# Two spectral-mixing and two GEGLU layers on one core: every pair of f tiles of w_down as seven block products

## The chip, the cores and the metric

The kernel is one program on one core of a Trainium2 chip. The metric is device time in microseconds (us) of one execution, as the median of several runs. Besides these runs one execution was recorded by the hardware profiler; all durations below that are not medians come from that execution.

The engines are named as in the profile: PE (TensorE's matrix multiplications), PEld (its weight loads), DVE (VectorE), ACT (ScalarE), POOL (GpSimd, which also issues DMAs) and SP (SyncE, which issues most DMAs).

## The reference

The input x has 2048 rows (S) and 512 columns (D), all in fp32. Four layers follow, each added to x after a layer norm without weights:

```python
def _A_ref(x, ...):              # Real(DFT_seq(DFT_hidden(x)))
    a = einsum("bsd,ed->bse", x, dft_hid_re)
    b = einsum("bsd,ed->bse", x, dft_hid_im)
    return einsum("ts,bse->bte", dft_seq_re, a) - einsum("ts,bse->bte", dft_seq_im, b)

def _B_ref(x, w_gate, w_up, w_down):          # F = 1792
    return (_gelu(x @ w_gate) * (x @ w_up)) @ w_down

x = x + _A_ref(_layernorm(x), ...)
x = x + _B_ref(_layernorm(x), ...)
x = x + _A_ref(_layernorm(x), ...)
x = x + _B_ref(_layernorm(x), ...)
```

## The kernel before

**Arithmetic.** An fp32 tile is split into a high and a low part (`split`: ACT copies to fp32r, DVE subtracts), and one product of two tiles is three matmuls: high times high, high times low, low times high (`mm3`, lines 175 to 177 of the profile). Each streams 512 columns through a 128x128 weight tile. Where a product can be cut in 2x2 blocks, the kernel takes seven block products and some sums in place of eight. The block products have names of their own: A11, A12, A22 of the weights themselves and S1 to S4 of sums of them.

**Layers.** `mix(layer)` for layers 0 and 2 goes over four column blocks b of the sequence transform, each in stages: A11 and A12 (for all four b first), then for each b S2 (which also makes S1 and S3), EARLY_HID, S4, MID_HID and LATE_HID. `six` is one block product of these stages: six matmuls, then one `step()`. `geglu(w, layer)` for layers 1 and 3 does half w of the rows (1024 rows, as two parts of 512). For each f tile n of 14, `up(n)` computes gate and up by block products, and GELU times up gives the hidden tile `h`. The product with w_down is either

* plain: for each f tile, part and 128 rows three matmuls (`down_steps`, `plain_rows`), that is 48 matmuls for a pair of f tiles, or
* by pairs: two neighbouring f tiles are one 2x2 block matrix with the two parts, and `down_product` does seven block products of six matmuls, that is 42 matmuls for a pair. A11 and A12 run beside `up` (`beside`), the others after it, in the order of `down_order`.

`SEVEN` says how many of the seven pairs of a layer and half are done by pairs. Before it is

```python
SEVEN = {(1, 1): 5, (3, 0): 7, (3, 1): 5}
```

so the half (layer 1, w 0) is plain altogether, (1, 1) and (3, 1) have five pairs and four plain f tiles, and (3, 0) has seven pairs.

**Rows.** A product by pairs yields transposed column blocks. `ended` closes an accumulation; `turned_rows` transposes on DVE and adds to the rows, which `load_turned` had loaded as `xwide` (part 0) and `wide` (part 1), and `rows_done` stores them with four DMAs a part. Where plain f tiles follow, the rows are stored to a buffer `begun` instead, loaded again in plain layout, and `plain_rows` adds the rest with `x_add`. After (1, 1) `plain_rows` keeps these tiles for the next layer norm (`keep`), so layer 2 does not load its second half of rows.

**Weights of the pairs.** `weight_steps(k, wdc, wdd)` loads pair k of w_down, makes four sums of 128x256 on DVE, splits four pieces and stores seven tiles to `wc`. Each product later loads its own tile from there (`s<-wc`). Before, pairs 0 and 1 are queued at the end of (1, 0), pairs 2 to 6 are made during `up` of (1, 1). The plain f tiles have split copies of their own (`wd`), made in (1, 0).

**What sets the order.** The kernel traces its work in one order: `queue` holds small steps of which each product runs one (`step`), `chores` are spread over the eight groups of a HID stage (`hid_groups`, `chores_at`), `slow` runs one step in nine. A stream of weight tiles (`items`, `take`) loads and splits a few items ahead. Tiles come from 94 slots of 128x512 (`s`), and the two wide tiles are lent to the same pool. The scheduler of the compiler then orders each engine's instructions. Within an engine the order is fixed: an instruction that waits holds up everything behind it on its engine.

Of the kernel before, what the change touches and what calls it, by code (L numbers as in the profile page):

```python
# [9 lines left out]
F32 = mybir.dt.float32  # L10
# [24 lines left out]
NSLOT = 94  # L35
SEVEN = {(1, 1): 5, (3, 0): 7, (3, 1): 5}
FORE = {0: 4, 2: 4}
MADE = 5
LEAD = 3
NK = NS // 2  # L40
# [6 lines left out]
def fnet_geglu(ctx: ExitStack, tc: tile.TileContext, x_in, ws, wh, wgu, wdn, wdc, out):  # L47
# [211 lines left out]

    items = []  # L260
    stream = {"loaded": 0, "split": 0, "used": 0, "more": 0}
    raws, parts = {}, {}

    def load_next():
        n = stream["loaded"]
        dtype, addresses, _, _ = items[n]
        raws[n] = []
        for a in addresses:
# [173 lines left out]
    for layer in range(0, 4, 2):  # L442
        mix_items(layer)
        for w in range(NB // 2):
            if (layer + 1, w) not in SEVEN:
                for part in range(2):
                    for f in range(NF):
                        if layer == w == part == 0:
                            items.append((F32, (wdn[f],), make_down_first(f), None))
                        else:  # L450
                            items.append((F32R, halves(wds[f]), whole, NEAR[0]))
            else:
                for near, products in zip(NEAR[1:], down_order(layer + 1, w)):
                    items.extend((F32R, (down_piece(k, name),), whole, near) for name, k in products)
                items.extend((F32R, halves(wds[f]), whole, NEAR[2]) for f in range(2 * SEVEN[layer + 1, w], NF))

# [207 lines left out]
    def mix(layer):  # L664
        hid, sums, chores, hid_left = {}, {}, [], [0]

        def chores_at(b):
            if b == NB - 3:
# [169 lines left out]
    def weight_steps(n, raw=wgu, place=wblocks):  # L838
# [19 lines left out]
        def divide(i):  # L858
            def run():
# [7 lines left out]
                if place is wblocks:  # L867
                    piece_here(n, i, t)
                else:
                    sb.put(*t)  # L870
                sb.put(src[i])
# [4 lines left out]
    def down_weight_steps(k):  # L876
        return weight_steps(k, wdc, wdd)

    down_making = {}
# [27 lines left out]
    def geglu(w, layer):  # L907
# [147 lines left out]
        def prepared(name, k):  # L1055

            if (name, k) in bs:
                return
            if k >= MADE:
                if name == "S1":  # L1060
                    second_made(k)
                elif name == "S2":
                    fourth_made(k)
            t = h4[k][PLACE[name]]
# [80 lines left out]

        def turned_rows(part, c, src):

            t = sb.get()
            blocks_of = "p (j e) -> p j e"
            nc.vector.transpose(t.rearrange(blocks_of, e=32), src.rearrange(blocks_of, e=32))  # L1150
            to = xturned[part].rearrange("p (j c e) -> p j c e", c=NT, e=32)[:, :, c]
            plus(to, to, t.rearrange(blocks_of, e=32))
            sb.put(t)

        def rows_done(part):
            rows_moved(layer + 1, part, lambda v, outside: nc.gpsimd.dma_start(outside, v))

        xrows = []
# [14 lines left out]
        def plain_rows():  # L1173
# [6 lines left out]
            for i in range(2 * NT):  # L1180
                part, n = divmod(i, NT)
                if part == 0:
                    ready(fs[n], 1)
# [44 lines left out]
        if w == 0:  # L1228
            queue.extend(others)
            if layer == 1:  # L1230
                down_making.update((k, down_weight_steps(k)) for k in range(2))
                queue.extend([down_making[0][0], down_making[1][0], *down_making.pop(0)[1]])
        elif before_mix:
# [19 lines left out]
        else:  # L1253
            if pairs == NP:
                pair_combined(NP - 1)
            late = down_order(layer, w)[1]
            for i, (name, k) in enumerate(late):
                for more in late[i:i + EARLY + 1]:
# [11 lines left out]
                while w == 0 and len(queue) > 2 * (len(late) - 1 - i):  # L1270
                    step()
            if pairs < NP:
                plain_rows()
# [4 lines left out]
        elif before_mix:  # L1278
            queue.extend([lambda k=k: combine_late(k) for k in range(NK)])

# [110 lines left out]
```

## Time and profile before

| | |
|---|---|
| median of 3 runs (lowest to highest) | 1619.23 us (1619.18 to 1620.68) |
| the profiled execution's own time | 1620.1 us |
| its span, first to last instruction | 1618.3 us |
| mean granted TensorE clock | 0.999 |
| busy share PE / DVE / ACT / POOL | 99% / 72% / 51% / 14% |
| DMA, read and written | 336.86 MB and 85.72 MB |

PE's busy time is a union of modelled, overlapping matmuls: it tells that PE rarely stands still, and the distance between the starts of two matmuls tells its pace. A row of the groups gives the source line, engine, operation, output<-input by the program's names, the shape, the count, then the busy time and the mean duration, then the engine's idle time ahead of these instructions and what ended it. A row of the windows has, for each engine, the busy time in this stretch and the instructions.

### The profile page before, as it was taken

To read this page: it belongs to the slowest core of one execution; us is meant where nothing else is said; L and a number is where in the kernel's file an instruction comes from. 1 tells how busy PE (TensorE), PEld (TensorE's weight loads), DVE (VectorE), ACT (ScalarE), POOL (GpSimd) and SP (SyncE) were. 2 spreads that over 40 slices of the span, in tenths; PEclk is the share of its full clock that TensorE was granted. 3 is DMA by queue.
4 is the path that set the end of the run, shared out by engine and by line. 5 is a ranking of instruction groups with operands and counts; after the bars stand their busy time and mean duration, and the time that the engine had idled before them with its cause. 6 is when DMAs were issued, how large, how long until landed. Compare 5 with 4: busy or idle time off the path is not lost.

```text
span 1618.3 us, 22864 instructions
## 1 busy us (share of the span) xinstructions
PE 1607.9 (99%) x7066; PEld 1325.5 (82%) x7066; DVE 1172.0 (72%) x2009; ACT 827.3 (51%) x1605; POOL 229.0 (14%) x421
## 2 busy tenths in 40 slices
PE   9999999999999999999999999999999999999998
PEld 6888888888888888888888888888888888888886
DVE  8999878888876655657877987887854547854573
ACT  7754454544775535557585434545445535433360
POOL 2101010203544022220131000100000000000002
PEclk9999999999999999999999999999999999999999
DMA  9858778799978799977858777777989676995455
GB/s 357 283 205 305 244 256 268 241 319 372 331 257 281 242 349 360 346 255 234 290 162 297 248 254 227 273 236 278 288 271 309 193 221 198 296 298 178 130 176 156
DMA packets 252106, 424.15 MB, mean 262 GB/s; under 512 B 28816, under 2 KB 91024, under 8 KB 250960
## 3 DMA queue, kind: packets, MB, share of 16 engines
q1 hardware_dynamic: 227232, 336.95, 65.1%
q0 software_dynamic: 24752, 85.74, 14.2%
q8 instruction: 56, 0.92, 0.3%
q14 instruction: 66, 0.54, 0.1%
HBM read 336.86 MB, written 85.72 MB: 261 GB/s over the span
## 4 chain that ended last, share of the span: by engine, by line
PE 95%; DMA 2%; DVE 1%; ACT 0%; issue 0%; POOL 0%; SPq 0%; POOLq 0%; DVEq 0%
PE p L177 32%; PE p L176 31%; PE p L175 31%; PE p L728 1%; DVE s L142 1%; DMA out<-s 1%; DMA s<-begun 0%; ACT s L141 0%; DMA begun<-xwide 0%; DMA s<-t 0%; DMA s<-x 0%; DVE s L166 0%; DVE s L1150 0%; DVE xwide L166 0%; DVE s L163 0%
## 5 line engine op out<-in xcount | busy, mean ns | idle before, releaser
L176 PE MATMUL p<-s,s 128*128 128x512 f32 x2334 | 907.5, 389 | 0.0
L177 PE MATMUL p<-s,s 128*128 128x512 f32 x2334 | 898.3, 389 | 0.4 <-DVE s L142 0.4
L175 PE MATMUL p<-s,s 128*128 128x512 f32 x2334 | 891.1, 389 | 0.1
L141 ACT ACTIVATE s<-s 128x512 fp32r<-128x512 f32 (+1 forms) x760 | 434.3, 606 | 387.1 <-DVE s L163 82.4
L142 DVE TENSOR_TENSOR s<-s,s 128x512 fp32r<-128x512 f32 (+1 forms) x760 | 481.0, 662 | 110.7 <-ACT s L141 82.2
L177 PEld LDWEIGHTS p<-s,s 128*128 128x128 f32 x2334 | 438.2, 188 | 92.7 <-DVE s L142 0.8
L175 PEld LDWEIGHTS p<-s,s 128*128 128x128 f32 x2334 | 438.2, 188 | 92.0 <-ACT s L141 1.0
L176 PEld LDWEIGHTS p<-s,s 128*128 128x128 f32 x2334 | 438.2, 188 | 92.0 <-issue 0.5
L166 DVE TENSOR_TENSOR s<-s,p 128x512 f32<-128x512 f32 x303 | 202.6, 682 | 176.4 <-PE p L177 94.1
L163 DVE TENSOR_TENSOR s<-s,s 128x512 f32<-128x512 f32 (+1 forms) x313 | 188.2, 614 | 16.3 <-DMA s<-ws 9.1
L170 ACT ACTIVATE s<-p 128x512 f32<-128x512 f32 x217 | 126.3, 591 | 120.1 <-PE p L177 117.9
L904 ACT ACTIVATE s<-s 128x512 f32<-128x512 f32 x104 | 65.4, 629 | 84.0 <-DVE s L166 82.5
L141 ACT ACTIVATE s<-xwide 128x512 fp32r<-128x512 f32 (+1 forms) x91 | 55.7, 618 | 54.2 <-PE p L176 22.3
L142 DVE TENSOR_TENSOR s<-xwide,s 128x512 fp32r<-128x512 f32 (+1 forms) x91 | 61.1, 676 | 21.8 <-ACT s L141 12.5
L498 POOL TENSOR_SCALAR rstd<-rstd 128x1 f32<-128x1 f32 x48 | 18.0, 376 | 388.7 <-ACT s L497 270.2
L166 DVE TENSOR_TENSOR s<-s,s 128x512 f32<-128x512 f32 (+1 forms) x61 | 37.4, 615 | 25.5 <-DMA s<-ws 14.3
L918 DVE TENSOR_TENSOR s<-s,s 128x512 f32<-128x512 f32 x77 | 53.1, 690 | 1.9
L257 POOL DMA_DIRECT2D wb<-s x84 | 45.7, 545 | 47.8 <-ACT s L141 28.7
L219 POOL DMA_DIRECT2D x<-s x43 | 23.5, 547 | 177.8 <-DVE s L166 176.3
L517 ACT ACTIVATE s<-s,shift,rstd 128x512 f32<-128x512 f32 x55 | 43.9, 808 | 7.2 <-DVE shift L490 6.2
L495 ACT ACTIVATE s<-s 128x512 f32<-128x512 f32 x39 | 24.3, 624 | 38.2 <-DMA s<-x 20.7
L599 DVE STREAM_TRANSPOSE wide<-s 128x512 f32<-128x512 f32 x29 | 20.3, 705 | 24.0 <-ACT s L517 24.0
(109 smaller groups left out, 524.8 us busy)
## 6 DMA issues: line engine op xcount, KB each, us to landing
s<-ws SPq DMA_DIRECT2D x375, 256.0 KB, 4.2
s<-wb SPq DMA_DIRECT2D x294, 256.0 KB, 4.6
s<-wc SPq DMA_DIRECT2D x119, 256.0 KB, 4.1
s<-wh SPq DMA_DIRECT2D x114, 256.0 KB, 4.9
wb<-s POOLq DMA_DIRECT2D x98, 256.0 KB, 4.5
s<-x SPq DMA_DIRECT2D x67, 256.0 KB, 4.9
xwide<-ws SPq DMA_DIRECT2D x56, 256.0 KB, 4.4
wc<-s POOLq DMA_DIRECT2D x49, 256.0 KB, 5.4
```

Of the source, the lines that this page charges most:

```text
L141: nc.scalar.activation(hi, src, AF.Copy)
L142: nc.vector.tensor_tensor(lo, src, f32(hi), op=ALU.subtract)
L163: nc.vector.tensor_tensor(out, a, b, op=ALU.subtract)
L166: nc.vector.tensor_tensor(out, a, b, op=ALU.add)
L170: nc.scalar.activation(v, src, AF.Copy)
L175: nc.tensor.matmul(ps, ah, bh, start=start, stop=False, skip_group_check=True)
L176: nc.tensor.matmul(ps, ah, bl, start=False, stop=False, skip_group_check=True)
L177: nc.tensor.matmul(ps, al, bh, start=False, stop=stop, skip_group_check=True)
L257: nc.gpsimd.dma_start(a, f32(t))
L517: nc.scalar.activation(z, x, AF.Identity, bias=shift, scale=rstd)
L904: nc.scalar.activation(t, g, AF.Gelu_apprx_tanh)
L918: nc.vector.tensor_tensor(t, t, v, op=ALU.mult)
```

## The change

All four entries of `SEVEN` become 7, so every pair of f tiles in both GEGLU layers and both halves is done by block products. With it:

* No plain f tile is left: `wd` is neither made nor loaded, and `plain_rows` and `begun` are not used any more.
* The weights of the pairs have to be ready for (1, 0). Pairs 0 and 1 are made among the chores of block b = 0 of layer 0 and pairs 2 and 3 among those of b = 1 (`BEFORE`, `down_chores`); pairs 4 to 6 during `up` of (1, 0).
* After (1, 1) the rows are stored by `rows_done` and loaded again for layer 2 from POOL's queue (`second_rows`). These steps and the sums that follow are spread over A11 and A12 of layer 2 (`GAPS`: empty steps between them).
* At the end of the program (`last_rows`) the product A22 runs one column block after the other: all seven pairs of block c = 0, then of c = 1, and each is transposed and added in two halves of 256; the rows leave in eight DMAs from SP as the halves are done.

```diff
-SEVEN = {(1, 1): 5, (3, 0): 7, (3, 1): 5}
+SEVEN = {(1, 0): 7, (1, 1): 7, (3, 0): 7, (3, 1): 7}
+BEFORE = {0: (0, 1), 1: (2, 3)}
+GAPS = 1, 2, 1
...
         def chores_at(b):
+            return (down_chores(*BEFORE.get(b, ())) if layer == 0 else []) + other_chores(b)
...
+    def down_chores(*ks):
+        steps = [down_weight_steps(k) for k in ks]
+        return [load for load, _ in steps] + [run for _, runs in steps for run in runs]
...
         def up(n):
-            if layer == 1 and w == 1:
+            if layer == 1 and w == 0:
                 k, odd = divmod(n + 3, 2)
-                if not odd and 2 <= k < NP:
+                if not odd and sum(map(len, BEFORE.values())) <= k < NP:
                     down_making[k] = down_weight_steps(k)
                     down_making[k][0]()
...
+        def last_rows():
+            ks, chain = range(pairs), banks["chain"]
+            ts = [take()[0] for _ in ks]
+            for k in ks:
+                prepared("A22", k)
+            for c in range(2):
+                for t, k in zip(ts, ks):
+                    weights = (t[:, h][:, c * P:(c + 1) * P] for h in half)
+                    mm3(chain[c], weights, bs["A22", k], False, k == pairs - 1)
+                for cut in half:
+                    turned_rows(0, 2 + c, chain[c], cut)
+                    if c:
+                        js = slice(cut.start // 32, cut.stop // 32)
+                        rows_moved(layer + 1, 0, lambda v, outside: nc.sync.dma_start(outside[:, js], v[:, js]))
...
-            queue.extend([lambda k=k: combine_late(k) for k in range(NK)])
+            if pairs == NP:
+                lend("x")
+                lend("z")
+                for k in (*range(NT, NK), *range(NT)):
+                    queue.extend([lambda k=k: second_rows(layer + 1, k), *[None] * GAPS[0]])
+                for k in range(NK):
+                    queue.extend([lambda k=k: combine(k), *[None] * GAPS[1]])
+            for k in range(NK):
+                queue.extend([lambda k=k: combine_late(k), *[None] * GAPS[2]])
```

PE's list gets shorter by 66 matmuls of 512 columns (7021 rows become 6955). Behind the added lines the line numbers are higher by 2 to 36: `mm3` is lines 177 to 179, the additions of line 166 are line 168, the transposes of line 1150 are line 1160. Three places show how the instructions move.

DVE in layer 0, block b = 0, between EARLY_HID and S4. Before, it holds splits (L142, L159) and the sums for the next S2 (L163, L166), all of 128x512:

```order
L159 SCALAR_TENSOR_TENSOR s_1902<-s_1691,s_1901 128x512
L166 TENSOR_TENSOR s_1869<-s_1867,s_1869 128x512
L142 TENSOR_TENSOR s_1928<-xwide,s_1927 128x512
L163 TENSOR_TENSOR s_1867<-s_1871,s_1867 128x512
L166 TENSOR_TENSOR s_1891<-s_1889,s_1891 128x512
```

In the changed kernel the same stretch has the four sums of one pair of w_down between them (128x256, on the tiles s_1747 to s_1750, which a DMA from `wdc` fills):

```order
L161 SCALAR_TENSOR_TENSOR s_1903<-s_1689,s_1902 128x512
L168 TENSOR_TENSOR s_1749<-s_1750,s_1749 128x256
L165 TENSOR_TENSOR s_1748<-s_1747,s_1750 128x256
L144 TENSOR_TENSOR s_1919<-xwide,s_1918 128x512
L168 TENSOR_TENSOR s_1892<-s_1890,s_1892 128x512
L161 SCALAR_TENSOR_TENSOR s_1925<-s_1691,s_1924 128x512
L165 TENSOR_TENSOR s_1748<-s_1749,s_1747 128x256
```

The sums of the weights now stand ahead of splits that PE needs for the next stages of layer 0.

POOL from the end of (1, 1) to the start of layer 2. Before, it stores `begun`, and then the tiles of `plain_rows` (x of layer 2), with no load:

```order
L1156 DMA begun_1_0_6741<-xwide 32x16x128 x4
L1156 DMA begun_1_1_6742<-wide 32x16x128 x4
L219 DMA x_2_94<-s_8757 128x512
L219 DMA x_2_94<-s_8759 128x512
L219 DMA x_2_94<-s_8761 128x512
```

In the changed kernel the rows themselves go out (x_3 is part 1, x_2 part 0) and come back on the same queue, with the terms of the norms (`rstd`) between them:

```order
L1166 DMA x_3_95<-wide 32x16x128 x4
L205 DMA s_8981<-x_3_95 128x512
L205 DMA s_9025<-x_3_95 128x512
L205 DMA s_9069<-x_3_95 128x512
L205 DMA s_9113<-x_3_95 128x512
L1166 DMA x_2_94<-xwide 32x16x128 x4
L499 TENSOR_SCALAR rstd<-rstd 128x1 x2
```

The eight loads of rows are new on this queue, and each group of four has to wait for the store ahead of it to land.

DVE at the end of the program. Before, the last instructions are additions of whole tiles from PSUM (p), each of which releases a store:

```order
L166 TENSOR_TENSOR wide<-wide,s_16542 128x16x32
L166 TENSOR_TENSOR s_16615<-s_16615,p_16657 128x512
L166 TENSOR_TENSOR s_16617<-s_16617,p_16672 128x512
L166 TENSOR_TENSOR s_16619<-s_16619,p_16687 128x512
L166 TENSOR_TENSOR s_16621<-s_16621,p_16702 128x512
```

In the changed kernel the last ones are transposes and additions of halves, first of one PSUM bank (p_15194, column block c = 0) and then of the other (p_15195, c = 1):

```order
L168 TENSOR_TENSOR wide<-wide,s_16705 128x16x32
L1160 STREAM_TRANSPOSE s_16763<-p_15194 128x256
L1160 STREAM_TRANSPOSE s_16766<-p_15194 128x256
L168 TENSOR_TENSOR xwide<-xwide,s_16763 128x8x32
L168 TENSOR_TENSOR xwide<-xwide,s_16766 128x8x32
L1160 STREAM_TRANSPOSE s_16790<-p_15195 128x256
L1160 STREAM_TRANSPOSE s_16797<-p_15195 128x256
L168 TENSOR_TENSOR xwide<-xwide,s_16790 128x8x32
L168 TENSOR_TENSOR xwide<-xwide,s_16797 128x8x32
```

The work behind the last matmul becomes four instructions on halves, and then the stores from `xwide`.

More of the change, by code (lines that the diff above doesn't have):

```diff
@@ L257, in kept @@
             nc.gpsimd.dma_start(a, f32(t))
-    items = []
+    items, needs, outside = [], {}, set()
     stream = {"loaded": 0, "split": 0, "used": 0, "more": 0}
@@ L267, in load_next @@
         raws[n] = []
+        assert n not in needs or needs[n] in outside
         for a in addresses:
@@ L444, in fnet_geglu @@
         for w in range(NB // 2):
[L445 to L455, printed above, removed]
+            for near, products in zip(NEAR[1:], down_order(layer + 1, w)):
+                for name, k in products:
+                    needs[len(items)] = k, next(i for i, names in enumerate(pieces) if name in names)
+                    items.append((F32R, (down_piece(k, name),), whole, near))
+            for f in range(2 * SEVEN[layer + 1, w], NF):
+                if layer == 0:
+                    items.append((F32, (wdn[f],), make_down_first(f), None))
+                else:
+                    items.append((F32R, halves(wds[f]), whole, NEAR[2]))
     queue, slow, steps_done = [], [], [0]
@@ L869, in run @@
                 else:
+                    outside.add((n, i))
                     sb.put(*t)
@@ L1058, in prepared @@
                 return
[L1059 to L1063, printed above, removed]
+            if name in ("S1", "S2") and len(h4[k]) == 4:
+                second_made(k)
+            if name == "S2" and k >= MADE:
+                fourth_made(k)
             t = h4[k][PLACE[name]]
@@ L1181, in plain_rows @@
                 part, n = divmod(i, NT)
-                if part == 0:
+                if part == 0 and n < len(fs):
                     ready(fs[n], 1)
@@ L1229, in geglu @@
             queue.extend(others)
-            if layer == 1:
-                down_making.update((k, down_weight_steps(k)) for k in range(2))
-                queue.extend([down_making[0][0], down_making[1][0], *down_making.pop(0)[1]])
         elif before_mix:
@@ L1256, in geglu @@
             late = down_order(layer, w)[1]
+            last = layer == 3 and w == 1
+            if last:
+                late = late[:-pairs]
             for i, (name, k) in enumerate(late):
@@ L1271, in geglu @@
                     step()
-            if pairs < NP:
+            if last:
+                last_rows()
+            elif pairs < NP:
                 plain_rows()
```

10 lines of the change are left out of this document (6 added, 4 removed).

## The prediction

> **What bounds the kernel now.** I read the page first, then PE's waits, then PE's timeline where its starts are not evenly spaced, then the groups and the windows of the stretches that the change touches, and last the chain at the end.
>
> The page: span, busy times, DVE in 40 slices, and the chain by engine:
>
> ```profile
> span 1618.3 us, 22864 instructions
> PE 1607.9 (99%) x7066; PEld 1325.5 (82%) x7066; DVE 1172.0 (72%) x2009; ACT 827.3 (51%) x1605; POOL 229.0 (14%) x421
> ...
> DVE  8999878888876655657877987887854547854573
> ...
> PE 95%; DMA 2%; DVE 1%; ACT 0%; issue 0%; POOL 0%; SPq 0%; POOLq 0%; DVEq 0%
> ```
>
> The chain that sets the end is PE from start to end. DVE comes next, and it is at 90% or more in the first mixing layer (slices 1 to 3) and around slice 19. The list of all that PE waited for is three rows long, which says that nearly every producer is early:
>
> ```profile
> PE p L1285 <- POOL ident masks.py:199: 1.4, 1, 1.4
> PE p L728 <- ACT s L517: 1.2, 1, 1.2
> PE p L177 <- DVE s L142: 0.4, 1, 0.4
> ```
>
> So a matmul that is not there any more is worth its distance to the next one. PE's timeline at the end, first and last of 13 matmuls in a row:
>
> ```profile
> 1607.85 0.39 PE L177 MATMUL p<-s,s 128*128 128x512 f32 x1
> ...
> 1610.57 0.39 PE L177 MATMUL p<-s,s 128*128 128x512 f32 x1
> ```
>
> Twelve distances in 2.72 us are 0.2267 us each. The 0.39 us is the latency of one matmul, and is not what is saved.
>
> **The change part by part.**
>
> *Fewer matmuls.* A pair costs 42 matmuls in place of 48, six less. New pairs are seven in (1, 0), two in (1, 1) and two in (3, 1): 11 x 6 = 66 matmuls, and PE's list shows just these 66 gone. 66 x 0.2267 = **-15.0 us**. The trace's 226.7 ns is used here. The Trainium skill's "TensorE: Matmul & The Clock Gate" (section "Wait — 56ns, not 53.3ns?") gives 215.7 ns between the starts of warm matmuls of 512 columns; by it, as an estimate, the term would be -14.2 us, and the trace is 5% slower than it.
>
> *plain_rows goes.* Two starts in it come late; and one at the hand-over from (3, 0), which already has seven pairs:
>
> ```profile
> 793.08 0.39 PE L177 MATMUL p<-s,s 128*128 128x512 f32 x1
> 793.52 0.50 PE L175 MATMUL p<-s,s 128*128 128x512 f32 x1
> ...
> 797.07 0.39 PE L176 MATMUL p<-s,s 128*128 128x512 f32 x1
> 797.88 0.50 PE L177 MATMUL p<-s,s 128*128 128x512 f32 x1 [0.42 <-DVE s L142]
> ...
> 1390.13 0.61 PE L175 MATMUL p<-s,s 128*128 128x512 f32 x2
> 1390.79 0.50 PE L176 MATMUL p<-s,s 128*128 128x512 f32 x1
> ```
>
> The first two gaps are 0.44 and 0.81 us, 0.8 us over the pace together, and go with `plain_rows`: **-0.8 us**. The third is 0.2 us over it (0.66 us for two matmuls less 0.45). (1, 0) gets the same hand-over: **+0.2 us**, and at most some 3 us, because DVE has more to do there (below).
>
> *The making of the weights moves.* Per pair it is three loads on SP, four half sums on DVE, three whole splits and a half one on ACT and DVE, and seven stores on POOL. The rows for the prices, then the windows of layer 0 from b = 0's S2 on, of (1, 0), of layer 2's A11 with A12, of its first S2, and of (3, 0):
>
> ```profile
> L142 DVE TENSOR_TENSOR s<-s,s 128x512 fp32r<-128x512 f32 x696 | 457.7, 684 | 104.7 <-ACT s L141 76.4 <-PE p L176 8.2 <-PE p L177 7.2
> L163 DVE TENSOR_TENSOR s<-s,s 128x256 f32<-128x256 f32 x83 | 33.2, 418 | 5.0 <-ACT s L517 4.6
> L166 DVE TENSOR_TENSOR s<-s,s 128x256 f32<-128x256 f32 x16 | 6.7, 420 | 11.0 <-DMA s<-wgu 7.9 <-DMA s<-wdc 3.2
> L141 ACT ACTIVATE s<-s 128x512 fp32r<-128x512 f32 x696 | 412.9, 625 | 380.3 <-DVE s L163 81.3 <-PE p L176 67.5 <-PE p L177 51.7
> ```
>
> ```profile
> 100.00:260.00 160.00, 160.00 (x708) 132.53 (x707) 141.75 (x233) 79.79 (x148) 18.20 (x35) 1.00 0.76 255
> 402.00:613.00 211.00, 211.00 (x933) 174.77 (x932) 144.22 (x258) 119.90 (x243) 72.57 (x138) 1.00 0.85 296
> 820.00:903.00 83.00, 83.00 (x367) 68.64 (x366) 66.72 (x123) 52.81 (x113) 16.91 (x22) 1.00 0.69 228
> 903.00:936.00 33.00, 33.00 (x147) 27.34 (x146) 30.80 (x52) 16.08 (x29) 1.08 (x2) 1.00 0.80 253
> 1208.00:1405.00 197.00, 196.95 (x870) 162.67 (x869) 120.82 (x190) 101.78 (x192) 7.42 (x17) 1.00 0.80 241
> ```
>
> Busy time by count gives what one costs in a dense queue: 457.7 / 696 = 0.66 us for a whole DVE operation, 0.40 for a half one, and 0.59 us for a whole one on ACT (a half one is taken at 0.40, too). A pair is 5 x 0.40 + 3 x 0.66 = 4.0 us of DVE, four pairs 16 us. The first sum also waits for the raw weights, and all of DVE's queue behind it with it: 11.0 us in 16 such rows, 0.7 us each, so 3 us for four. That makes 19 us. From 100 to 260 us DVE has 160 - 141.75 = 18.2 us free, and PE does not wait there. The work just fits, and what is late spills into the stretch after it, where the page's slices show 80%. POOL (18 of 160 us busy) takes 28 stores of 0.52 us (18.20 / 35), and the 9 MB of DMA are 57 GB/s on top of 255, below the peaks that the trace has elsewhere (296 as a mean over (1, 0)). I take **0**; the bounds are 0 and the second rival.
>
> *(1, 0) and (1, 1).* Seven pairs in (1, 0) need 11 whole DVE operations each (four sums, seven splits): 51 us; three pairs are made there: 12 us. The plain version's 28 splits of `h` and 14 of w_down (28 us) and the making of two pairs (8 us) go. DVE goes from 144 of 211 us to 171 of about 202. (3, 0) runs the same product code without a real gap, at 121 of 197. **0**, at most the 3 us named. (1, 1) loses the making of five pairs, and gains nothing but two pairs. SP's list has 77 loads from `wc` more, and 44 from `wd` and 14 of w_down less, of 256 KB each; (3, 0) shows the loads from `wc` hidden.
>
> *Rows come back from outside.* The same trip stands in the chain of the last stage:
>
> ```profile
> 1586.66 0.29 POOL begun L1156
> ...
> 1595.02 3.18 DMA s<-begun
> ...
> 1598.30 0.70 DVE s L166
> ```
>
> From the first store to the first use it takes 11.6 us. In the new order 175 matmuls, 39.7 us, lie between the last A22 product and the first A12 product of layer 2, which wants these rows; product k = 7 is 42 matmuls later, 49.2 us in all. ACT has 66 whole and 16 half operations in these 49.2 us: 66 x 0.59 + 16 x 0.40 = 45 us. DVE has 144 whole and 48 half ones up to the end of the first S2, 511 matmuls or 115.8 us: 144 x 0.66 + 48 x 0.40 = 114 us. Both fit, without room. Nothing in the trace shows this fit itself; the nearest row is the window 903 to 936, where DVE is busy for 30.8 of 33 us and PE does not wait. Between 0 and 7.6 us (first rival) I take **+1.0 us**.
>
> *The end.* The DMA issues' sizes and times to landing (stores of plain rows, loads of turned ones), the transpose out of PSUM among the groups, and two runs of four issues in SP's timeline:
>
> ```profile
> out<-s SPq DMA_DIRECT2D x8, 256.0 KB, 4.4
> xwide<-x SPq DMA_DIRECT2D x21, 256.0 KB, 8.0
> ```
>
> ```profile
> L1150 DVE STREAM_TRANSPOSE s<-p 128x512 f32<-128x512 f32 x6 | 4.2, 715 | 10.8 <-PE p L177 10.8
> ```
>
> ```profile
> 1357.84 1.83 SPq L613 DMA_DIRECT2D s<-t  x4
> 1611.63 3.71 SPq L219 DMA_DIRECT2D out<-s  x4
> ```
>
> Before, the last matmul ends at 1610.57 + 0.39 = 1610.96, and the span ends 7.4 us later. After the change, DVE's halves for column block c = 0 fit beside the 21 matmuls (4.8 us) of c = 1. Behind the last matmul come two half transposes and a half addition. A half transpose is not in the trace; it lies between the half addition's 0.40 and the whole transpose's 0.72, and 0.40 is taken, since the whole one costs as much as a whole addition: 3 x 0.40 = 1.2 us. Then SP issues eight DMAs, each in 1.83 / 4 = 0.46 us (at most in 3.71 / 4 = 0.93, where the issues also wait). The last one starts at 1.2 + 7 x 0.46 = +4.4 and lands 4.4 us later: +8.8 us, **+1.4 us** more than before. With a landing of 3.2 us as that of `s<-begun` above it is +0.2; with issues of 0.93 and a landing of 8.0 it is 1.2 + 6.5 + 8.0 = 15.7, +8.3. I stay near the low end, since nothing else is queued on SP by then.
>
> **Sum.** -15.0 - 0.8 + 0.2 + 1.0 + 1.4 = -13.2 us. The profiled execution took 1620.1 us (span 1618.3) and would take 1606.9; the median, 0.9 us below it, comes to 1619.23 - 13.2 = **1606.0 us**. The forecast's own range is 1603.5 to 1610: all terms at their good ends give -15.6, and the tail halfway to its bad end, or the hand-over at its 3 us with 1 us more at layer 2, gives 1609 to 1610.
>
> **The rivals.**
>
> 1. *DVE or ACT is the bound at the start of layer 2.* The 114 us of DVE work have 115.8 us only if DVE is never idle. It can run ahead by seven split tiles (`AHEAD`), 4.6 us, while it waits for rows; if it stands idle for the trip of 11.6 us and 2.4 us of transposes ahead of it, PE loses 114 + 14 - 115.8 - 4.6 = 7.6 us. For it: 114 of 115.8 us is a full queue. Against it: part 1's rows leave about 40 matmuls earlier in the new order, and give DVE work meanwhile. Time: 1606.0 - 1.0 + 7.6 = 1612.6, or 1613. "TensorE: Matmul & The Clock Gate" in the Trainium skill ("What's actually happening") says that about 3.4 us of idle PE halve its clock until it was busy as long again; a whole stall would then cost 1.7 us more, 1614.3, by estimate. The windows above show a clock of 1.00 throughout, and no wait there is that long. Chance 0.13.
> 2. *Slower: DVE in layer 0.* The sums of w_down stand in DVE's queue ahead of the splits of layer 0. Among all waits the one for `wgu`, in the same sums, shows in total, times and longest what a late load costs:
>
> ```profile
> DVE s L166 <- DMA s<-wgu: 7.9, 3, 3.4
> ```
>
>    If each of the four pairs waits for the longest, 3.4 us, they take 16 + 13.6 = 29.6 us of DVE. If also none of the 18.2 free us can be used (DVE is free then because its inputs are not there), all of it reaches PE: 1606.0 + 29.6 = 1635.6. It decides the sign once more than 13.2 us reach PE. Against it: 18.2 us free beside a PE that never waits are at least partly a full lead. Chance 0.07: 0.04 slower than the bound, 0.03 near no change.
> 3. *(1, 0) is short of DVE* at the hand-over, 171 of 202 us with the making in its dense half: +3 to +4 us, 1610. Chance 0.06.
>
> That the change does not do what it says is ruled out by PE's list.
>
> **How the numbers follow.** The forecast has 0.74. A measurement of this kernel can tell 0.2%, 3.2 us, from no change; only the second rival comes near. Faster: 0.74 + 0.13 + 0.06 = 0.93; same 0.03; slower 0.04. The range reaches from 1603.5 to the first rival's 1613.
>
> **What would show it.** Right: 66 matmuls less at 0.227 us, PE's waits still under 3 us in total, the last landing 8 to 10 us behind the last matmul, no `begun`, and a span near 1605. Wrong: a row of PE waiting for DVE or ACT behind 780 us (first rival) or between 130 and 260 us (second), a slice with a lower granted clock, or a tail over 12 us.

## The result and the profile after

| | before | after |
|---|---|---|
| median (lowest to highest), 12 runs each | 1619.12 us (1618.5 to 1621.88) | 1619.88 us (1616.7 to 1621.8) |
| the profiled execution | 1620.1 us | 1617.54 us |

After to before is 1.0001, with a 95% interval of 0.9993 to 1.0009: the change is worth nothing that can be measured, where 1606.0 us were predicted. The 66 matmuls did go. Here are, from the page of the changed kernel, its span and busy times, and then the list of all that PE waited for (total, times, longest):

```profile
span 1615.8 us, 22819 instructions
PE 1596.0 (99%) x7000; PEld 1312.4 (81%) x7000; DVE 1199.9 (74%) x2074; ACT 829.3 (51%) x1630; POOL 209.1 (13%) x381
```

```profile
PE p L177 <- ACT s L172: 4.9, 4, 2.1
PE p L177 <- DVE s L168: 2.4, 2, 2.1
PE p L1321 <- POOL ident masks.py:199: 1.4, 1, 1.4
PE p L732 <- ACT s L518: 1.1, 1, 1.1
PE p L177 <- ACT s L143: 0.8, 1, 0.8
PE p L178 <- DVE s L144: 0.2, 1, 0.2
```

Before, this list came to 3.0 us, and now it comes to over 10. (The line numbers are higher than before: the splits are L143 and L144, sums L165 and L168, copies out of PSUM L172, the three matmuls L177 to L179.) PE's timeline has the three longest of the new waits:

```profile
361.64 0.39 PE L179 MATMUL p<-s,s 128*128 128x512 f32 x1
364.18 0.50 PE L177 MATMUL p<-s,s 128*128 128x512 f32 x1 [2.15 <-DVE s L168]
...
417.14 0.39 PE L179 MATMUL p<-s,s 128*128 128x512 f32 x1
419.29 0.50 PE L177 MATMUL p<-s,s 128*128 128x512 f32 x1 [1.76 <-ACT s L172]
...
436.87 0.39 PE L179 MATMUL p<-s,s 128*128 128x512 f32 x1
439.33 0.50 PE L177 MATMUL p<-s,s 128*128 128x512 f32 x1 [2.07 <-ACT s L172]
```

Below, a *gap* is a distance between two starts less the pace of 0.2267 us. (Where the granted clock is at half, see the last section, every matmul has such a gap, of 0.2 us.) From 36 us on, the gaps above 0.12 us sum to 1.0 us before and to 10.6 us after: 4.1 us at the end of layer 0 (340 to 395 us), 5.8 us at the start of (1, 0) (395 to 470 us), and 0.7 us at the start of layer 2. So the loss stands in the two stretches where the prediction had put 0.

**End of layer 0.** POOL stores the turned norms there in one DMA (`t<-wide`, 1 MB). The timelines of POOL and SP, then the DMA issues between 320 and 345 us (their last number is the time to landing), of the kernel before:

```profile
320.81 0.54 POOL L602 DMA_DIRECT2D t<-wide  x1
...
323.05 3.10 SPq L235 DMA_DIRECT2D s<-m  x2
328.38 1.82 SPq L613 DMA_DIRECT2D s<-t  x2
```

```profile
t<-wide POOLq DMA_DIRECT2D x1, 1024.0 KB, 7.5
```

The same of the kernel after:

```profile
324.66 0.54 POOL L603 DMA_DIRECT2D t<-wide  x1
...
326.94 1.75 SPq L237 DMA_DIRECT2D s<-m  x2
334.83 2.38 SPq L276 DMA_DIRECT2D s<-ws  x5
```

```profile
t<-wide POOLq DMA_DIRECT2D x1, 1024.0 KB, 10.1
```

SP's queue stands still until that store has landed, before and after: 320.81 + 7.5 = 328.3, and 324.66 + 10.1 = 334.8. SP's list of waits says the same, first before, then after:

```profile
SPq L613 <- DMA t<-wide: 2.2, 1, 2.2
```

```profile
SPq L276 <- DMA t<-wide: 6.1, 1, 6.1
```

It goes on 6.4 us later than before, because the store is issued 3.9 us later and takes 2.6 us longer. The next five loads of raw weights are behind it, and from 341 us on PE waits. The stop alone doesn't cost: in the run e9 below it is 5.0 us long, ends at 329.4 us, and no gap follows.

What came ahead of it can be read from the windows (the last two numbers are the DMA engines' share and GB/s), before and after. The 28 stores of the pairs' weights (`wc<-s`) are issued from 126 to 170 us and from 206 to 243 us.

```profile
160.00:200.00 40.00, 40.00 (x178) 33.15 (x177) 35.28 (x58) 17.45 (x29) 2.16 (x4) 1.00 0.76 248
240.00:260.00 20.00, 20.00 (x90) 16.56 (x89) 17.97 (x31) 9.71 (x17) 2.16 (x4) 1.00 0.86 311
260.00:280.00 20.00, 20.00 (x90) 16.57 (x89) 14.64 (x23) 5.88 (x11) 0.00 (x0) 1.00 0.82 235
```

```profile
160.00:200.00 40.00, 40.00 (x178) 33.14 (x177) 37.71 (x64) 20.30 (x36) 7.00 (x13) 1.00 0.89 320
240.00:260.00 20.00, 20.00 (x90) 16.57 (x89) 13.86 (x23) 12.42 (x32) 9.16 (x16) 1.00 0.98 335
260.00:280.00 20.00, 20.00 (x90) 16.58 (x89) 19.84 (x34) 12.61 (x24) 1.62 (x3) 1.00 0.95 356
```

From 240 to 280 us the DMA engines' share is 0.95 to 0.98. DVE is busy less in the first 20 us (13.86 for 17.97), with one wait of 3.0 us for raw weights (`ws`), and then has no free time in the next 20 (19.84 of 20).

**Start of (1, 0).** SP's timeline after the change, and two waits from the timelines of DVE and ACT:

```profile
398.54 11.64 SPq L214 DMA_DIRECT2D s<-x  x12
410.28 0.91 SPq L853 DMA_DIRECT2D s<-wgu  x1
411.24 0.62 SPq L854 DMA_DIRECT2D s<-wgu  x1
411.96 5.48 SPq L1153 DMA_DIRECT2D xwide<-x  x4
417.48 4.12 SPq L214 DMA_DIRECT2D s<-x  x4
...
422.17 3.84 SPq L1153 DMA_DIRECT2D xwide<-x  x4
```

```profile
416.73 0.42 DVE L168 TENSOR_TENSOR s<-s,s 128x256 f32<-128x256 f32 x1 [4.15 <-DMA s<-wgu]
...
436.63 0.63 ACT L143 ACTIVATE s<-s 128x512 fp32r<-128x512 f32 x1 [7.00 <-DMA s<-wgu]
```

An issue takes about 1 us there (11.64 us for 12), where single ones between 430 and 436 us take 0.33 us; the DMA engines' share from 396 to 420 us is 1.03. The eight `xwide<-x` are the transposed rows of part 0 (`load_turned`). They belong at the end of `up`, but nothing in the program holds them back, and the scheduler puts them at the start of (1, 0), among the raw gate/up weights (`wgu`). These land late, and DVE and ACT wait for them. The copies out of PSUM (L172) at 437.17 and 438.69 us, for which PE waits, stand behind such a wait in ACT's queue. For the first wait shown, of 4.15 us, the rows' place in the queue is not the reason: its weights were issued at 410.28 and 411.24 us, ahead of the rows and behind twelve other loads (`s<-x`).

The rows of part 0 are 1 MB, four DMAs of 256 KB. There are eight because the program calls `load_turned(0)` twice in a half with seven pairs: in `beside` at n = 13, and again behind the loop over `up`. Both write the one buffer `xwide`, and the products that are added to these rows (A12 and A22) end behind the second call, so nothing reads the first four. (3, 0) has the same eight, before the change too. No run leaves out the repeated ones alone.

### The profile page after: what moved, and what is told of

Read it like the earlier page. It is cut to its first block, busy times and chain, and to the rows that moved or that the text cites. A ratio compares the mean times of both kernels' runs of the same rounds, so it can differ in the third digit from the quotient of the medians.

```text
span 1615.8 us, 22819 instructions
## 1 busy us (share of the span) xinstructions
PE 1596.0 (99%) x7000; PEld 1312.4 (81%) x7000; DVE 1199.9 (74%) x2074; ACT 829.3 (51%) x1630; POOL 209.1 (13%) x381
## 5 line engine op out<-in xcount | busy, mean ns | idle before, releaser
L179 PE MATMUL p<-s,s 128*128 128x512 f32 x2312 | 894.6, 390 | 0.0
L177 PE MATMUL p<-s,s 128*128 128x512 f32 x2312 | 876.1, 390 | 8.2 <-ACT s L172 4.9
L143 ACT ACTIVATE s<-s 128x512 fp32r<-128x512 f32 (+1 forms) x792 | 444.4, 606 | 369.8 <-DVE s L165 154.9
L144 DVE TENSOR_TENSOR s<-s,s 128x512 fp32r<-128x512 f32 (+1 forms) x792 | 499.1, 667 | 71.1 <-ACT s L143 68.1
L177 PEld LDWEIGHTS p<-s,s 128*128 128x128 f32 x2312 | 433.9, 188 | 103.2 <-ACT s L172 7.1
L179 PEld LDWEIGHTS p<-s,s 128*128 128x128 f32 x2312 | 434.1, 188 | 90.8 <-issue 0.7
L168 DVE TENSOR_TENSOR s<-s,p 128x512 f32<-128x512 f32 x299 | 201.1, 685 | 201.5 <-PE p L179 107.0
L165 DVE TENSOR_TENSOR s<-s,s 128x512 f32<-128x512 f32 (+1 forms) x369 | 225.2, 626 | 18.0 <-DMA s<-ws 15.2
L172 ACT ACTIVATE s<-p 128x512 f32<-128x512 f32 x234 | 136.8, 591 | 135.1 <-PE p L179 133.6
L914 ACT ACTIVATE s<-s 128x512 f32<-128x512 f32 x112 | 70.2, 629 | 122.1 <-DVE s L168 119.5
L143 ACT ACTIVATE s<-xwide 128x512 fp32r<-128x512 f32 (+1 forms) x81 | 49.2, 616 | 30.1 <-DVE xwide L168 10.7
L168 DVE TENSOR_TENSOR s<-s,s 128x512 f32<-128x512 f32 (+1 forms) x70 | 42.9, 615 | 26.5 <-DMA s<-ws 19.2
L144 DVE TENSOR_TENSOR s<-xwide,s 128x512 fp32r<-128x512 f32 (+1 forms) x81 | 54.9, 686 | 0.5 <-ACT s L143 0.3
L1166 POOL DMA_DIRECT2D out<-wide x8 | 5.2, 654 | 281.9 <-DVE wide L168 280.9
L496 ACT ACTIVATE s<-s 128x512 f32<-128x512 f32 x40 | 24.8, 622 | 29.1 <-DMA s<-x 29.1
```

The lines of the kernel that those rows point to most:

```text
L143: nc.scalar.activation(hi, src, AF.Copy)
L144: nc.vector.tensor_tensor(lo, src, f32(hi), op=ALU.subtract)
L165: nc.vector.tensor_tensor(out, a, b, op=ALU.subtract)
L168: nc.vector.tensor_tensor(out, a, b, op=ALU.add)
L172: nc.scalar.activation(v, src, AF.Copy)
L177: nc.tensor.matmul(ps, ah, bh, start=start, stop=False, skip_group_check=True)
```

## Experiments

Two theories. **M**: the making of four pairs in layer 0 is the loss there, and perhaps all that follows. **R**: the loads of transposed rows at the start of (1, 0) are the loss there. A rival to both: the order that the scheduler happened on, or the product itself, is short of an engine in (1, 0). Ratios are to the kernel before on the same chip; 0.001 is 1.6 us. The gaps are those of one profile each. The changed kernel itself, profiled three times (the first row and the last two), has 4.1 to 6.8 us of them to 395 us, and 2.4 to 6.8 us from there to 470 us, so a difference of some 3 us between two kernels there says little. A stretch at half clock counts in them too: some 1.0 to 1.8 us in each of e1, e8, e10, e13, e15 and e16, and 6 us in e2. All gaps are counted from 36 us on.

| kernel | median us | ratio (95% interval) | gaps to 395 | 395 to 470 | later |
|---|---|---|---|---|---|
| after | 1619.9 | 1.0001 (0.9993 to 1.0009) | 4.1 | 5.8 | 0.7 |
| e1_no_making | 1612.1 | 0.9962 (0.9951 to 0.9974) | 0.9 | 5.7 | 2.4 |
| e5_no_rows_10 | 1614.1 | 0.9960 (0.9947 to 0.9972) | 5.2 | 1.2 | 1.2 |
| e9_neither | 1606.9 | 0.9920 (0.9906 to 0.9933) | 0 | 0 | 0.9 |
| e8_making_bare | 1616.7 | 0.9982 (0.9972 to 0.9991) | 4.2 | 2.7 | 0.5 |
| e10_no_stores | 1613.4 | 0.9965 (0.9953 to 0.9978) | 0 | 5.5 | 1.2 |
| e4_spread | 1613.3 | 0.9966 (0.9955 to 0.9978) | 2.7 | 3.7 | 0.2 |
| e6_three_ahead | 1607.1 | 0.9923 (0.9911 to 0.9936) | 0 | 0.4 | 2.5 |
| e11_three_bunched | 1609.9 | 0.9943 (0.9929 to 0.9956) | 0 | 2.4 | 1.6 |
| e12_three_no_rows | 1606.2 | 0.9923 (0.9911 to 0.9936) | 0 | 0 | 4.0 |
| e13_raw_earlier | 1620.6 | 1.0000 (0.9991 to 1.0008) | 8.1 | 2.0 | 3.9 |
| e14_three_earlier | 1613.3 | 0.9956 (0.9944 to 0.9968) | 0 | 2.1 | 3.0 |
| e2_rows_later | 1631.7 | 1.0081 (1.0068 to 1.0095) | 6.9 | 8.3 | 11.7 |
| e3_10_plain | 1618.0 | 0.9992 (0.9984 to 1.0001) | 0.2 | 2.5 | 2.3 |
| e7_end_alone | 1618.3 | 0.9994 (0.9985 to 1.0002) | 0 | 0.5 | 0.7 |
| e15_look (after, again) | 1619.8 | a single run | 4.7 | 6.8 | 1.1 |
| e16_look (after, again) | 1618.2 | a single run | 6.8 | 2.4 | 1.4 |

**e1: layer 0 makes nothing.**

```diff
-            return (down_chores(*BEFORE.get(b, ())) if layer == 0 else []) + other_chores(b)
+            return other_chores(b)
 # down_piece:
+        if k < 4:
+            t = whs[k % 2, i]
...
```

> Left out: the making of the first four pairs of w_down in layer 0 (8 loads of 256 KB and 8 of 128 KB, 16 sums, 16 splits, 28 stores); the products of these pairs read bytes of another table of the same size, so DMA counts in layer 1 stay. Theory M (the making in layer 0 eats the lead of the splits, and everything PE waits for from 340 to 456 us follows from it): the 12 us of gaps in that stretch go, about 1608 us. Theory R (the gaps at the end of layer 0, 4.7 us, come from the making, but those at the start of (1,0), 6.8 us, come from the loads of transposed rows and x that are issued there ahead of raw gate/up weights): about 1615 us, gaps at 417 and 437 us stay. If the gain is lost elsewhere: 1620 us.

The layer's gaps fell from 4.1 to 0.9 us, and those of (1, 0) stayed at 5.7 (1.2 of them at half clock): the pattern of R, with M for layer 0 alone. The time fell by 0.0039 of 1619 us, 6.3 us, more than the 3.2 us by which the layer's gaps fell in one profile.

**e5: the rows aren't loaded. e9: neither.**

```diff
 # load_turned (e5; e9 has this and the edit of e1):
+            if layer == 1 and w == part == 0:
+                nc.gpsimd.memset(xturned[part], 0.0)
+                return
             rows_moved(layer, part, lambda v, outside: nc.sync.dma_start(v, outside))
```

> Left out: the load of the transposed rows for part 0 of (1,0) (eight DMAs of 256 KB at its start); the tile is set to zero on POOL instead, so x isn't added there. All else as in the changed kernel. Theory R (these loads hold up the raw gate/up weights behind them): the gaps from 395 to 470 us fall from 5.8 us to under 1 us, and the time to 1614 to 1615 us. If the start of (1,0) is short for another reason (too many DMAs of every kind at once, or the order that the scheduler happened on): gaps of 4 to 6 us stay there, 1618 to 1620 us.

> Left out: both the making in layer 0 (as in e1) and the load of the transposed rows at the start of (1,0). If M and R together are the loss: gaps from 36 us on under 3 us in all, 1606 to 1608 us, the predicted time. If the start of (1,0) is short for another reason: 1610 to 1612 us, with 4 to 6 us of gaps from 395 to 470 us.

e5: the gaps from 395 to 470 us fall to 1.2 us, all of it at 418.9 us, where the changed kernel has its first one there; and the time falls by 0.0041, 6.6 us. e9: 0.0081, 13.1 us, where 6.3 and 6.6 add up to 12.9; the time is 1606.9 us, and all gaps together are 0.9 us. So the making of the four pairs and the rows' loads are the whole loss; how the rows cost is a question of its own (e12 below). Its windows have PE at the full pace (116 matmuls in 26 us, 90 in 20):

```profile
340.00:366.00 26.00, 26.00 (x116) 21.55 (x115) 21.57 (x36) 11.36 (x20) 0.00 (x0) 1.00 0.91 259
...
420.00:440.00 20.00, 20.00 (x90) 16.57 (x89) 18.03 (x36) 14.02 (x33) 10.62 (x16) 1.00 0.76 259
```

The changed kernel in the same windows:

```profile
340.00:366.00 26.00, 22.70 (x95) 17.01 (x94) 19.62 (x33) 11.35 (x21) 0.00 (x0) 1.00 0.92 262
...
420.00:440.00 20.00, 17.93 (x80) 14.52 (x79) 12.96 (x22) 10.13 (x22) 4.96 (x9) 1.00 1.09 315
```

**e8 and e10: what of the making costs.** e8 leaves out the arithmetic and keeps the traffic, e10 the other way round.

```diff
 # weight_steps, for n < 4 and place wdd
 # e8:
+        if place is not wblocks and n < 4:
+            return load, [bare(i) for i in range(len(pieces))]    # only stores src[0]
         return load, [sums] + [divide(i) for i in range(len(pieces))]
 # e10, in divide (and the products of these pairs read another table):
-                    kept(to, t)
+                    if here:
+                        kept(to, t)
```

> The making of the first four pairs in layer 0 keeps its loads (6 MB), its 28 stores and its waits for the loads at the stores, but its 16 sums and 16 splits are left out: raw bytes are stored. Theory M as work of DVE and ACT: the gaps from 340 to 395 us (4.1 us) go as they do without any making (0.9), and the time comes to 1612 to 1613 us. Theory M as DMA traffic or slots: the gaps stay, 1618 to 1620 us.

> The making in layer 0 keeps its loads, its 16 sums and its 16 splits; its 28 stores of 256 KB (7 MB) are left out, and the products of these four pairs read another table of the same size. Without the whole making the changed kernel took 1612.1 us, without its sums and splits 1616.7. If the rest of its cost is the traffic of the stores, on POOL's queue and the DMA engines: about 1615 us (-4.5), with gaps under 2 us from 340 to 395 us. If it is the loads and the order of the queues: 1619 to 1620 us, with 4 us of gaps there.

First row e8's window, second row e10's:

```profile
340.00:366.00 26.00, 23.53 (x97) 18.89 (x97) 19.51 (x32) 11.82 (x21) 0.00 (x0) 0.93 0.95 266
```

```profile
340.00:366.00 26.00, 26.00 (x116) 21.56 (x115) 20.43 (x34) 11.22 (x21) 0.00 (x0) 1.00 0.93 240
```

Without the 32 sums and splits the layer's gaps stay, at 4.2 us (one wait of 2.6 us, and a stretch at half clock behind it); without the 28 stores they go, with all the arithmetic in place. The store of the turned norms is issued at 324.4 us in e8, as in the changed kernel, and at 320.4 us in e10, as before. The DMA engines' share from 240 to 260 us, 0.98 in the changed kernel, is 0.83 in e10. In time the stores are worth 0.0036 (5.8 us) and the arithmetic 0.0019 (3.1 us), against 6.3 us for the whole, so the two overlap; where the arithmetic's part is lost isn't shown. (e8's time lies between its two numbers, and e10's 1.6 us below its expectation.) At the end of layer 0 the cost is that of the stores. Their traffic is the likely way, but leaving them out also frees slots and POOL's queue earlier, and no run tells these apart. (The loads of the four pairs are 2 MB in the trace, eight DMAs of 128 KB and four of 256 KB; the expectations of e1 and e8 have 3 and 6 MB.)

**e4, e6, e11: how many pairs, and where.**

```diff
-BEFORE = {0: (0, 1), 1: (2, 3)}
+BEFORE = {0: (0,), 1: (1,), 2: (2,), 3: (3,)}   # e4
+BEFORE = {0: (0,), 1: (1,), 2: (2,)}            # e6
+BEFORE = {0: (0, 1), 1: (2,)}                   # e11
```

> One pair of w_down is made in each of the four blocks of layer 0 rather than two in each of the first two. Theory M in the form that the bunching counts: the gaps shrink by some 3 to 5 us, 1615 to 1617 us. Theory M in the form that the sum of the work counts: 1620 us, with gaps at the end of layer 0 as before or larger, since the last two blocks also make gate/up weights and norms. Theory R: the gaps at the start of (1,0) stay at 6 to 7 us.

> Pairs 0, 1 and 2 are made in blocks 0, 1 and 2 of layer 0, one each; pairs 3 to 6 in (1,0). If layer 0 is where the time goes: the fourth pair's 4 us of DVE leave it, 1611 to 1612 us, under 2 us of gaps from 340 to 395 us. If (1,0) is short of DVE, the gap comes back there: 1614 to 1617 us, with PE waiting between 400 and 500 us for more than the 3.7 us of the kernel with one pair in each block.

> Three pairs ahead as in the kernel that took 1607.1 us, but pairs 0 and 1 both in block 0 and pair 2 in block 1 of layer 0. If the amount of making in layer 0 decides (three pairs fit, four don't): 1607 to 1609 us. If bunching in the first two blocks decides: 1612 to 1616 us, with PE gaps again between 340 and 395 us, behind a late store of the turned norms.

Both count, though the intervals of e6 and e11 just overlap. Four pairs spread out gain 0.0035; three pairs bunched, 0.0058; three spread out, 0.0078, and the latter, with nothing left out, beats both kernels: 1607.1 us, 0.9923 of the time before (0.9911 to 0.9936). e4 came out 2 us below its expectation and e6 4 us, and e11 between its two numbers. In e6 the store of turned norms is issued only at 334.5 us, and SP's stop there (3 us, 340.29 to 343.27) is put down to a load of weights (`wh`) and not to the store: a late store doesn't cost by itself either, and what matters is which loads stand behind it. That (1, 0) would run short of DVE with one pair more was not seen.

**e12 and e14: e6 without the rows' load; e6 with raw weights a step earlier.** e13 is the latter edit on the changed kernel.

```diff
+            making[3][0]()
-            if n + 3 in making:
-                making[n + 3][0]()
+            if n + 4 in making:
+                making[n + 4][0]()
```

> Three pairs ahead, one in each of the first three blocks (1607.1 us), and the load of the transposed rows at the start of (1,0) left out (zeros on POOL instead, so x isn't added for part 0). In the changed kernel that load cost 5.8 us. If it is hidden once layer 0 hands over in time: 1606 to 1607 us, no difference. If it costs there too: 1602 to 1604 us.

> The changed kernel, with the raw gate/up weights of each step in (1,0) loaded four steps ahead rather than three; nothing is left out, and the transposed rows are loaded as before, now behind these weights in SP's queue. If the load costs by its place in the queue: the gaps from 395 to 470 us fall from 5.8 us to under 1.5 us, those at the end of layer 0 stay, and the time is 1614 to 1615 us. If it costs by its traffic (DMA engines full from 396 to 440 us): the gaps stay at 4 to 6 us, 1618 to 1620 us.

> Three pairs ahead, one in each of the first three blocks of layer 0 (1607.1 us), and raw gate/up weights four steps ahead. That kernel has 2.9 us of gaps left, 0.4 of them from 395 to 470 us: 1606 to 1607 us, no difference. If the slots that the earlier weights hold are missed elsewhere: 1609 us or more.

In e12 the same load that cost 6.6 us in e5's place costs nothing that can be told. In e13 the gaps of (1, 0) fall to 2.0 us with the load whole, but this tells nothing: e16, the changed kernel itself, has 2.4 us there and 6.8 us in layer 0, and the time of e13 is that of the changed kernel (gaps of 8.1 us in layer 0, and 2.5 us from 575 to 600 us). e14 shows that the earlier weights cost something by themselves: 2.5 us of gaps from 569 to 590 us, and 0.0033 (5.3 us) in time against e6, where no difference, or 2 us and more, were expected. So whether the rows cost by their place in SP's queue or by their traffic stays open, and that they cost depends on the order that they meet: the rival of the scheduler's order isn't ruled out for (1, 0). What hides them in e6 stays open too: its start of (1, 0) has DMA engines as full (share 1.05), and DVE waits longer for `wgu` there, 9.2 us for 7.2, with 0.4 us of gaps on PE.

**e2: rows later by an explicit tie.**

```diff
-            rows_moved(layer, part, lambda v, outside: nc.sync.dma_start(v, outside))
+            with tc.issue_after(stream["last"].ins):
+                rows_moved(layer, part, lambda v, outside: nc.sync.dma_start(v, outside))
```

> The loads of the transposed rows (eight DMAs of 256 KB in 512-byte pieces) may be issued only behind the last weight load that precedes them in program order, in all four halves. Theory R: the gaps at the start of (1,0) go (6.8 us), about 1613 us. Theory M: no change, 1619 to 1620 us, and the raw gate/up weights still land late there.

Neither theory's number: 12 to 13 us slower than the changed kernel. The tie was made in all four halves, and the scheduler moved much else with it: gaps grew in layer 0, whose code is the same, and new ones of 4.7 and 5.1 us, each with a stretch at half clock in it, stand at 577 to 592 and 1376 to 1387 us, in the last third of (1, 0) and of (3, 0). It decides nothing on R; e5 shows that the rows cost here.

**e3 and e7: the smaller parts.** e3 leaves (1, 0) plain, e7 is the kernel before with the change in (3, 1) alone.

```diff
+SEVEN = {(1, 1): 7, (3, 0): 7, (3, 1): 7}           # e3, with layer 0 making nothing
+SEVEN = {(1, 1): 5, (3, 0): 7, (3, 1): 7}           # e7, with last_rows
```

> (1,0) stays the plain product and layer 0 makes nothing; (1,1), (3,0) and (3,1) have seven pairs, rows come back from outside, the last column blocks end one by one: 24 of the 66 matmuls go. Both M and R: 1619.1 - 5.4 - 0.8 + 0.9 (start of layer 2) + 1.5 (end) = 1615.3 us, with under 2 us of PE gaps from 340 to 456 us. If something in the rest of the change eats the gain (return of rows, end): 1619 us or more.

> The kernel before, with the change in (3,1) alone: seven pairs there and the last column blocks ending one by one. 12 matmuls less are -2.7 us, the gap at its plain rows -0.2, the end +1.4 as predicted: 1617.6 us for 1619.1 before. If the end is dearer than that (a tail over 12 us): 1620 us or more.

e3 gained 1.3 us of the 3.8 expected, and its interval includes no gain: 2.5 us of gaps stand from 395 to 470 us and 1.7 us at 665 us, though (1, 0) is as before; what puts them there isn't settled. e7 gained 1.0 us of 1.5, within the interval.

**e15 and e16: the scatter of the changed kernel.** Its profiled execution has a mean granted clock of 0.998, and its others from 0.996 to 0.998.

> The changed kernel as it is, profiled again. If its slower runs lose to the clock: where the time is over 1619 us, the trace has one or two stretches of 3.4 us at half clock (1.7 us each), each behind a PE gap of over 2 us between 340 and 456 us. If they lose to longer waits: no such stretch, and the sum of the gaps is larger by the same amount.

> As e15_look: the changed kernel once more. With a time of 1617 to 1618 us no stretch at half clock; over 1619 us one or two, if the clock is the cause.

They took 1619.8 us (clock 0.996) and 1618.2 us (0.997). e15's windows, the granted clock third from the right, and PE's timeline:

```profile
418.00:422.00 4.00, 0.97 (x5) 0.47 (x3) 1.16 (x3) 0.00 (x0) 0.21 (x1) 0.89 1.06 342
422.00:428.00 6.00, 4.60 (x11) 3.63 (x12) 3.96 (x8) 3.87 (x8) 0.67 (x2) 0.50 1.16 237
428.00:432.00 4.00, 4.00 (x20) 3.28 (x19) 2.27 (x4) 3.28 (x7) 1.59 (x4) 1.00 1.23 198
```

```profile
423.40 0.80 PE L177 MATMUL p<-s,s 128*128 128x512 f32 x1 [4.43 <-ACT s L172]
424.00 0.63 PE L178 MATMUL p<-s,s 128*128 128x512 f32 x1
424.42 0.63 PE L179 MATMUL p<-s,s 128*128 128x512 f32 x1
```

Behind a wait of 4.43 us the matmuls start 0.43 us apart. The records have one stretch of 6.83 us at half clock in e15, and one of 3.41 us in e16, behind a gap of 2.95 us at 362 us, where none was expected for a time near 1618 us. By these figures a stretch of 3.41 us costs up to half its length, 1.7 us, and lowers the mean clock by 0.0011 (an estimate). So the clock is part of what the slower runs lose, but not all: e15's longest gap, in which its stretch begins, is itself longer: 4.6 us at 418.6 us, for 1.9 us at 417.1 us in the first profile.

## Why the prediction was wrong, step by step

* **Fewer matmuls, -15.0 us; plain_rows, -0.8 us: right.** 7000 matmuls for 7066, and no gap between 470 and 905 us. e9, which has all of PE's work in the new form and neither of the two costs, took 1606.9 us for 1606.0 predicted.
* **Hand-over of (1, 0), +0.2 us: right.** No gap is there. **Start of layer 2, +1.0 us (first rival 7.6): right in size, by a pick.** The 1.0 was chosen between two bounds, so that it fits is in part luck. It has the only gaps behind 470 us, 0.7 us:

```profile
908.00 0.39 PE L179 MATMUL p<-s,s 128*128 128x512 f32 x1
908.47 0.50 PE L177 MATMUL p<-s,s 128*128 128x512 f32 x1
...
909.04 0.40 PE L179 MATMUL p<-s,s 128*128 128x512 f32 x1
909.67 0.50 PE L177 MATMUL p<-s,s 128*128 128x512 f32 x1 [0.23 <-DVE s L168]
```

* **The end, +1.4 us: right in sum, in part by luck.** The timeline from PE's last matmul on, then the DMA issues behind 1600 us with the time to landing:

```profile
1606.66 0.39 PE L179 MATMUL p<-s,s 128*128 128x512 f32 x1
1607.08 0.78 DVE L1160 STREAM_TRANSPOSE s<-p 128x256 f32<-128x256 f32 x2 [2.88 <-PE p L179]
1607.79 0.72 DVE L168 TENSOR_TENSOR xwide<-xwide,s 128x256 f32<-128x256 f32 x2
1608.20 4.38 SPq L1182 DMA_DIRECT2D out<-xwide  x8
```

```profile
out<-xwide SPq DMA_DIRECT2D x8, 128.0 KB, 2.4
```

  The span ends 1615.77 - 1607.05 = 8.7 us behind PE, for 8.8 predicted. A half transpose takes 0.39 us (0.40 taken). Two terms were off, and one was missing: the eight issues are 0.55 us apart (0.46 taken), which adds 0.7 us to the last one; a landing takes 2.4 us, 2.0 less than the 4.4 taken; and the span ends about 1.3 us behind the last landing, which the sum didn't have. These three cancel.
* **The making of the weights, 0 us ("The work just fits"): wrong by about 6 us.** The step that failed is the one on DMA: "57 GB/s on top of 255, below the peaks that the trace has elsewhere". It set a mean over 160 us against a mean over 211 us, and its sum, 312, is above the 296 that it named. Over the 160 us the rate went to 287 GB/s; the rest of the traffic came later. In the four windows between 131 and 260 us where the stores fall, the engines' share was already 0.75 to 0.90, and with them it is 0.81 to 0.98; in the next 20 us it is 0.95 for 0.82. For DVE the sum was less wrong: e8 shows that the layer's gaps stay without the sums and splits, though leaving these out gains 3.1 us in time. The second rival named the layer, but for another reason (late raw weights holding DVE), and looked for waits between 130 and 260 us. The loss is made there, and PE's waits show it only from 341 us on.
* **(1, 0), 0 us ("at most the 3 us named"): wrong by about 6.6 us.** Its DVE work was summed, and (3, 0) taken as the model. The step that failed is this summing up: it has no term for the eight loads of transposed rows, four of them needless, which (1, 0) didn't have before, and which nothing ties to the place where the program asks for them. (3, 0) makes no gate/up weights in its first steps; in (1, 0) these share SP's queue and the DMA engines with the rows. The 6.6 us (e5) are what the rows cost in this order; in that of e6 they cost nothing (e12), and why is open.
* **The range** (1603.5 to 1613.0) had no case in which two costs taken at 0 come together, about 13 us in all (e9); the highest was one rival alone.


## What to carry to other kernels

Cost a moved step in the stretch where it lands, for the DMA engines as for the compute engines: here seven more megabytes went where the share was 0.75 to 0.90, and a mean over 160 us didn't show it. List the DMAs that a new code path issues, and ask for each whether it is needed, and what keeps it from being issued too early: an early load may hold up one that is needed at once, and whether it does depends on the order (6.6 us in one here, nothing in another). And a lead that shrinks without a wait is a cost that may come due later, where a store or load holds up a queue.

## What was not expected of the hardware

The stretches at half clock last 3.41 us, and start on a fixed grid. Counted from where PE first has the full clock they start at 131.0 (e1), 99.0 (e8), 121.0 (e10) and 106.0 (e13) times 3.413 us. Take PE's idle time (the gaps above) and sum it in each cell of this grid, up to the last matmul. Then every cell with 2.1 to 2.9 us of idle time (eleven, in e1, e2, e8, e10, e13, e15 and e16) is followed by one at half clock, and none with up to 2.0 us is, in all eighteen profiles. No cell lies between. So a single wait of 2.3 us may cost up to 1.7 us more (half a cell, an estimate), or nothing where it lies across the border of two cells, as the one at 361.64 us in the profiled execution of the changed kernel.

"TensorE: Matmul & The Clock Gate" in the Trainium skill ("What's actually happening") says that the clock falls to half behind at least one idle window of about 3.4 us, and that these windows run freely. The trace agrees with the windows and their length; but a window with 2.1 us of idle time was enough here, not only one that is idle throughout.
